# A spectral mix and a gated FFN on one core: half of the down projection by seven products, and a first product multiplied one step early

## The chip, the cores and the metric

The kernel runs on one core of a Trainium2 chip. The metric is the device time of one execution in microseconds (us). An engine is named by its short name: PE is TensorE, PEld its weight loads, ACT is ScalarE, DVE is VectorE, POOL is GpSimd, SP is SyncE, which here only issues DMAs.

## The reference, cut to what matters

Two stages follow each other. All arithmetic that the output sees is fp32.

```python
X = rfft(x, axis=1)                       # x: 8 batches x 3008 positions x 256
Yr = X.real @ w_r - X.imag @ w_i + b_r;  Yi = X.real @ w_i + X.imag @ w_r + b_i
Y  = softshrink(Yr, 0.01) + 1j * softshrink(Yi, 0.01)
y  = irfft(Y, n=3008, axis=1)             # 24064 tokens x 256
h  = y @ w_in                             # w_in: 256 x 2048
out = (h * sigmoid(1.702 * h)) @ w_out    # w_out: 2048 x 256
```

## The kernel before

**Numbers.** An fp32 operand is split into a high and a low part of a shorter format (`split`, L131: a cast on ACT, a subtraction on DVE), and a product of two operands is three matmuls into one PSUM bank (`mm3`, L134: high by high, high by low, low by high). This text calls such three matmuls a *product*.

**The spectral stage** (`spectral`, L256) makes y batch by batch: stage A, stage B, the mix with w_r and w_i, the inverse. Batch 0 is done ahead of the loop, in plain fp32. The first stages of batches 1 and 2 are a list called `filler`, taken two pairs at a time by `fill`. Everything later stands in `queue`, as steps with a cost each; the main loop takes the next step whenever the share of the costs spent lags behind the share of the way covered (L638). `tokens` (L425) turns y into tokens by features, eight small matmuls at a time, as soon as the loop will need them (L642).

**The FFN** is the main loop (L603). Tokens come in 24 tiles of 1024 (the last has 512), and the 2048 hidden features in eight blocks of 256: 192 steps, `k` the tile and `q` the block. In a step, the up projection of 256 hidden features from 256 inputs for 2 halves of 512 tokens is a 2 by 2 by 2 block product, and it is done with seven products instead of eight, by Winograd's form of Strassen's method. The seven turned weights of a block are made once, on DVE and ACT (`up_weights`, L220), stored in DRAM (`kept`), and loaded again for each later tile (`load_up`, L246). The seven token operands are made once per tile (`Tile`, L444). `Step.up` (L492) issues the products 1, 5, 6, 2, 7, 4, 3: products are added up in two banks, and ACT copies intermediate sums (`saved`, L478) that DVE adds to a later bank (`block`, L482, the addition in L486). Each of the four blocks of h gets its gate on ACT (L487) and is split.

The down projection of a step is eight plain products (`Step.down`, L518), accumulated over the eight steps of a tile in four PSUM banks `po`, which are copied out once per tile (L528). The downs of a step are multiplied during the step behind it. Four further PSUM banks (`bank()`) are shared by the up products and all of the spectral stage.

**The order** on each engine comes from a list scheduler that places instructions by the order of the program and by when buffers and operands come free in its own timeline; on the chip each engine's queue then runs in that fixed order. The order of the program around the change is set by one tuple, in which a number is an up product and 0 is one down product of the step before:

```python
PATTERN = (1, 5, 0, 6, 2, 0, 7, 0, 0, 4, 0, 3, 0, 0, 0)
```

The DMAs of the loop are all issued from SP; POOL issues the loads of the raw float64 weights (`from_float64`, L180).

## Time and profile before

| | us |
|---|---|
| median of 3 runs | 2602.62 (2600.95 to 2603.32) |
| the profiled execution | 2600.49 |
| span in its trace | 2598.4 |
| PE busy | 2550.3 (98%) |
| PE weight loads busy | 2129.2 (82%) |
| ACT busy | 1779.9 (69%) |
| DVE busy | 1551.5 (60%) |
| DMA moved | 376.33 MB, 145 GB/s |

The span runs from the first to the last instruction of the trace; the other 2.1 us of the profiled execution lie around it. Matmuls overlap in the trace: each is shown for longer than the distance to the start of the next, so what a matmul costs in a row of them is read from the starts. The same holds, in a smaller measure, for ACT and DVE.

### The profile page before, as it was taken

The numbers are of one execution on the slowest core, as the hardware profiler recorded it, in microseconds if no ns is written. First come the engines' busy times: TensorE is split into PE (matmuls) and PEld (weight loads), VectorE is DVE, ScalarE is ACT, GpSimd is POOL, SyncE is SP. The second block draws the span as 40 slices with busy tenths as digits, with TensorE's granted clock in tenths as the row PEclk, the third lists the DMA queues.
The fourth block names the chain that finished last, engine by engine and source line by source line (L and its number), as shares of the span: only waits on it lengthen the run. The fifth ranks groups of instructions, "written<-read, shape, count | busy, mean of one in ns | idle before, by whom it ended". The sixth has DMA issues, their size and how long they took to land.

```text
span 2598.4 us, 35299 instructions
## 1 busy us (share of the span) xinstructions
PE 2550.3 (98%) x12765; PEld 2129.2 (82%) x12765; DVE 1551.5 (60%) x2550; ACT 1779.9 (69%) x3309; POOL 13.8 (1%) x25
## 2 busy tenths in 40 slices
PE   6999999999999999999999999999999999999999
PEld 3768888888788888888878888788888888888888
DVE  5756665655556656566555665556656666455545
ACT  4577666666767668677676766767777676666667
POOL 1000000000000000000000000000000000000000
PEclk8899999999999999999999999999999999999999
DMA  9674544333544446343363444634355433433233
GB/s 298 196 228 131 166 133 132 128 122 118 177 133 138 131 135 201 128 141 125 128 201 115 140 127 152 193 105 144 120 171 168 131 126 117 137 121 120 86 105 124
DMA packets 183997, 376.33 MB, mean 145 GB/s; under 512 B 21808, under 2 KB 109232, under 8 KB 183824
## 3 DMA queue, kind: packets, MB, share of 16 engines
q1 hardware_dynamic: 181440, 365.70, 43.9%
q0 software_dynamic: 2384, 8.39, 1.1%
q8 instruction: 101, 1.65, 0.3%
q14 instruction: 72, 0.59, 0.1%
HBM read 266.52 MB, written 82.31 MB: 134 GB/s over the span
## 4 chain that ended last, share of the span: by engine, by line
PE 90%; DMA 5%; ACT 2%; DVE 1%; issue 1%; SPq 0%; ACTq 0%; POOL 0%; POOLq 0%
PE pa L135 15%; PE pa L136 14%; PE pa L137 14%; PE po L135 13%; PE po L136 12%; PE po L137 12%; PE pa L430 4%; PE pa L330 3%; DMA xr<-in_x 2%; PE pa L349 1%; PE pa L297 1%; DMA s<-aev 1%; DMA wraw<-in_w_in 1%; DMA yr<-mv 1%; ACT g L487 1%
## 5 line engine op out<-in xcount | busy, mean ns | idle before, releaser
L132 DVE TENSOR_TENSOR gl<-g,gl 128x512 fp32r<-128x512 f32 (+1 forms) x768 | 514.4, 676 | 336.1 <-ACT gl L132 333.4
L136 PE MATMUL po<-gl,wo_h 128*128 128x512 f32 (+1 forms) x1536 | 594.6, 388 | 0.0
L137 PE MATMUL po<-gl,wo_l 128*128 128x512 f32 (+1 forms) x1536 | 590.4, 385 | 0.0
L486 DVE TENSOR_TENSOR g<-pa,s 128x512 f32<-128x512 f32 (+1 forms) x576 | 387.0, 677 | 317.1 <-PE pa L137 227.5
L135 PE MATMUL pa<-tk,wq 128*128 128x512 f32 (+1 forms) x1344 | 536.7, 400 | 5.5 <-ACT iev L391 1.9
L136 PE MATMUL pa<-tk,wq 128*128 128x512 f32 (+1 forms) x1344 | 520.9, 388 | 0.0
L137 PE MATMUL pa<-tk,wq 128*128 128x512 f32 (+1 forms) x1344 | 518.8, 386 | 0.0
L487 ACT ACTIVATE g<-g 128x512 f32<-128x512 f32 (+1 forms) x576 | 358.3, 624 | 216.4 <-DVE g L486 214.3
L135 PE MATMUL po<-gl,wo_h 128*128 128x512 f32 (+1 forms) x1536 | 486.4, 390 | 1.6 <-ACT gl L132 1.2
L480 ACT COPY s<-pa 128x512 f32<-128x512 f32 (+1 forms) x576 | 330.0, 578 | 214.8 <-PE pa L137 208.9
L132 ACT CAST gl<-g 128x512 fp32r<-128x512 f32 (+1 forms) x768 | 464.0, 613 | 10.3
L136 PEld LDWEIGHTS po<-gl,wo_h 128*128 128x128 f32 x1536 | 288.9, 188 | 56.8 <-DVE gl L132 0.6
L137 PEld LDWEIGHTS po<-gl,wo_l 128*128 128x128 f32 x1536 | 288.8, 188 | 56.4 <-issue 0.7
L135 PEld LDWEIGHTS po<-gl,wo_h 128*128 128x128 f32 x1536 | 279.7, 188 | 58.2 <-ACT gl L132 6.3
L135 PEld LDWEIGHTS pa<-tk,wq 128*128 128x128 f32 x1344 | 254.0, 189 | 65.0 <-ACT s L480 8.4
L137 PEld LDWEIGHTS pa<-tk,wq 128*128 128x128 f32 x1344 | 253.4, 189 | 52.7 <-issue 0.5
L136 PEld LDWEIGHTS pa<-tk,wq 128*128 128x128 f32 x1344 | 254.3, 189 | 46.4 <-issue 2.9
L487 ACT ACTIVATE g<-pa 128x512 f32<-128x512 f32 (+1 forms) x192 | 112.8, 588 | 63.7 <-PE pa L137 62.3
L430 PEld LDWEIGHTS pa<-kc,ur 96*128 96x128 f32 x1024 | 139.5, 198 | 14.9 <-ACT we L200 2.7
L135 PE MATMUL pa<-wf_h,zh 128*128 128x256 f32 x504 | 143.4, 285 | 0.4 <-ACT g L487 0.3
L137 PE MATMUL pa<-wf_h,zl 128*128 128x256 f32 x504 | 142.4, 283 | 0.0
L136 PE MATMUL pa<-wf_l,zh 128*128 128x256 f32 x504 | 142.4, 282 | 0.0
(99 smaller groups left out, 2537.5 us busy)
## 6 DMA issues: line engine op xcount, KB each, us to landing
wq<-kept SPq DMA_DIRECT2D x184, 896.0 KB, 4.8
s<-aev SPq DMA_DIRECT2D x128, 192.0 KB, 3.1
br<-s SPq DMA_DIRECT2D x96, 256.0 KB, 3.3
yr<-mv SPq DMA_DIRECT2D x384, 64.0 KB, 2.0
s<-iev SPq DMA_DIRECT2D x96, 256.0 KB, 2.4
ur<-s SPq DMA_DIRECT2D x128, 192.0 KB, 3.4
out<-o SPq DMA_DIRECT2D x92, 256.0 KB, 2.8
xr<-in_x SPq DMA_DIRECT2D x80, 192.0 KB, 3.5
```

What stands on the lines that cost most here:

```text
L132: return nc.scalar.copy(hi, src).ins, nc.vector.tensor_tensor(lo, src, hi.bitcast(F32), ALU.subtract).ins
L135: nc.tensor.matmul(ps, lhsT=wh, rhs=xh, start=start, stop=False, skip_group_check=more)
L136: nc.tensor.matmul(ps, lhsT=wh, rhs=xl, start=False, stop=False, skip_group_check=more)
L137: nc.tensor.matmul(ps, lhsT=wl, rhs=xh, start=False, stop=stop, skip_group_check=more)
L297: done_a.append(nc.tensor.matmul(ps[:96], lhsT=ka32, rhs=xs.pop(q), start=True, stop=True).ins)
L330: nc.tensor.matmul(pv[:, c, :, i], lhsT=t[:, i, cs], rhs=k[:, i], start=True, stop=True)
L349: nc.tensor.matmul(ps, lhsT=z[:, 3 * c + v], rhs=wf32[v][:, c], start=c == 0, stop=c == 1)
L430: turned.append(nc.tensor.matmul(pv[:, c, 94 * j:94 * j + 94], lhsT=t[:, j, 128 * c:128 * c + 128], rhs=kz, start=True, stop=True).ins)
L480: nc.scalar.copy(t, ps[:, :self.w])
L486: nc.vector.tensor_tensor(t, ps[:, :w], self.s[other], ALU.add)
L487: nc.scalar.activation(t, ps[:, :w] if other is None else t, AF.Gelu_apprx_sigmoid)
```

## The change

Blocks 0 to 3 of the hidden features (`NF = 4`, a *fast* step) get a down projection by seven products; blocks 4 to 7 keep the eight plain ones.

- In a fast step, DVE makes four sums of the gated blocks (`block`: f5, f6, f7, f4). Four of the seven products (1, 5, 6, 7) are multiplied as the step's downs. Their sums over the four fast steps stand in the four `po` banks.
- After the downs of step 3 the banks are turned (`Tile.turn`): four copies on ACT and four additions on DVE, with PSUM as source and destination, combine the four banks.
- The other three products (2, 3, 4) go straight into the turned banks. Their operands are kept in fp32 (`held`, a pool of 12 buffers), and split and multiplied one fast step at a time among the downs of the plain steps 4 to 7 (`tile.solo`), which thus have 11 products.
- The downs of a step are still multiplied during the next one, so the pattern has two forms: with four downs (`FEW`, in steps 1 to 4) and with eleven (`MANY`, in steps 5, 6, 7 and 0).
- The up products come in the order 1, 6, 2, 5, 7, 3, 4. Product 1 of a step is multiplied within the step in front of it, and ACT copies it from its bank into the bank that the step in front has just emptied (a PSUM to PSUM copy); product 2 is added onto it there. One addition on DVE per step is gone with that, and the bank goes on being used.
- Turned weights of w_out for the fast blocks are made, stored and loaded like those of w_in, in halves (`HALVES`: u, v of w_in, d, e of w_out; four tiles of buffers for halves of four, four for halves of three).
- The costs of the spectral queue are spread unevenly over the steps of a tile (`SHARE`), and tokens are wanted between steps 4 and 6.9 of a tile, where it was 2.5 to 6.5.
- The copies out of the four banks are made together after the last down of a tile (`Tile.finish`).

```diff
+NF = 4
+TK, GL, G, WQ, DF = 7, 6, 5, 4, 3 * NF
+HALVES = {"u": (1, 6, 2, 5), "v": (7, 3, 4), "d": (1, 5, 6, 7), "e": (2, 3, 4)}
...
+    def load_turned(h, n):
         k, q = divmod(n, NQ)
+        if k < NT and (k or h == "e") and q < (NF if h in "de" else NQ):
+            nc.sync.dma_start(flat(new_turned(k, h, q)), kept[h, q])
...
+        def turn(self):
+
+            c11, c12, c21, c22 = (self.bank(m, n) for m in range(2) for n in range(2))
+
+            def add(to, ps):
+                t = buf2("tn").rearrange("p c d -> p (c d)")[:, :self.w]
+                nc.scalar.copy(t, ps)
+                for o in to:
+                    nc.vector.tensor_tensor(o, o, t, ALU.add)
+
+            add((c12,), c11)
+            add((c21,), c12)
+            add((c12,), c22)
+            add((c22,), c21)
...
         def block(self, name, ps, other=None):
             w = self.w
-            t = buf([128, TOK], F32, "g", bufs=G)[:, :w]
+            t = held(w) if self.fast and name[0] else buf([128, TOK], F32, "g", bufs=G)[:, :w]
             if other is not None:
                 nc.vector.tensor_tensor(t, ps[:, :w], self.s[other], ALU.add)
             nc.scalar.activation(t, ps[:, :w] if other is None else t, AF.Gelu_apprx_sigmoid)
...
+            if not self.fast:
+                self.cut(name, t)
+            elif name == (0, 0):
+                self.cut(1, t)
+            elif name == (0, 1):
+                f[5], f[6] = (buf([128, TOK], F32, "g", bufs=G)[:, :w] for _ in range(2))
+                v.tensor_tensor(f[5], t, f[0, 0], ALU.subtract)
+                self.cut(5, f[5])
+                v.tensor_tensor(f[6], f[1, 1], f[5], ALU.subtract)
+                self.cut(6, f[6])
+                v.tensor_tensor(t, t, f[1, 1], ALU.subtract)
+                self.cut(7, t)
+            elif name == (1, 0):
+                f[4] = held(w)
+                v.tensor_tensor(f[4], f[6], t, ALU.subtract)
 
         def up(self, p):
+            w = self.w
             if p == 1:
                 self.a = bank()
                 self.product(1, self.a, True, True)
-                self.saved("p1", self.a)
+                if self.b is None:
+                    self.saved("p1", self.a)
+                else:
+                    nc.scalar.copy(self.b[:, :w], self.a[:, :w])
             elif p == 5:
                 self.c = bank()
                 self.product(5, self.c, True, True)
+                self.saved("p5", self.c)
+            elif p == 2:
...
+                    self.product(2, self.b, False, True)
+                    self.block((0, 0), self.b)
             elif p == 6:
                 self.product(6, self.a, False, True)
                 self.saved("u2", self.a)
+            elif p == 3:
+                self.product(3, self.c, False, True)
+                self.block((0, 1), self.c, "u2")
             elif p == 7:
                 self.product(7, self.a, False, True)
-                self.saved("u3", self.a)
-                self.block((1, 1), self.c, "u3")
+                self.block((1, 1), self.a, "p5")
...
+    BLOCKS = ((0, 0), (0, 1), (1, 1), (1, 0))
+    FEW = (6, 2, 0, 5, 7, 0, 3, 1, 0, 4, 0)
+    MANY = (6,0,2,0,5,0,7,0,0,3,0,0,0,4,0,1,0,0)
+    SHARE = (1.6,.3,.3,.3,.5,1.6,1.7,1.7)
...
+        if n < NF - 1:
+            turn_weights(1, n + 1, True)
+        if n < NQ - 3:
+            turn_weights(0, n + 3, True)
+        if q < NF:
+            load_turned("d", n)
+        else:
+            load_turned("e", n - NF)
+        load_turned("u", n + 2)
+        load_turned("v", n + 2)
...
+        pattern = FEW if 1 <= q <= NF else MANY
+        for i, p in enumerate(pattern):
+            if p == 1:
+                if n + 1 < NT * NQ:
+                    follow = Step(coming if last else cur, (q + 1) % NQ, step)
+                    follow.up(1)
+            elif p:
                 step.up(p)
                 if last:
                     coming.factor(p)
-            elif behind:
-                behind.pop(0)()
+            else:
+                next_down()
```

## Rows read from the trace of the kernel before

**Rows 1.** The page's first part: the span, then busy time and share of it for each engine, with instructions.

```profile
span 2598.4 us, 35299 instructions
PE 2550.3 (98%) x12765; PEld 2129.2 (82%) x12765; DVE 1551.5 (60%) x2550; ACT 1779.9 (69%) x3309; POOL 13.8 (1%) x25
```

**Rows 2.** The page's fourth part: the chain of work that ended last, by engine.

```profile
PE 90%; DMA 5%; ACT 2%; DVE 1%; issue 1%; SPq 0%; ACTq 0%; POOL 0%; POOLq 0%
```

**Rows 3.** Busy time by stretches. The first four are each about one tile of the main loop, from its first up product on: the first tile, one in the middle, one of those behind the last batch's spectral work, and the last, of half the width. The fifth is the last step of the first tile. Columns: the stretch and its length, busy us (instructions) of PE, PEld, DVE, ACT and POOL, granted clock, DMA share, GB/s.

```profile
127.70:259.70 132.00, 129.38 (x588) 95.81 (x587) 85.20 (x163) 95.14 (x184) 2.15 (x4) 0.98 0.56 179
1229.40:1342.40 113.00, 109.87 (x533) 89.90 (x532) 65.77 (x106) 80.04 (x150) 0.00 (x0) 1.00 0.48 150
2290.30:2376.40 86.10, 86.10 (x401) 72.02 (x400) 44.46 (x69) 56.75 (x103) 0.00 (x0) 1.00 0.33 110
2545.30:2598.40 53.10, 49.21 (x383) 47.71 (x381) 27.10 (x65) 36.29 (x97) 0.00 (x0) 0.98 0.40 135
...
239.80:259.70 19.90, 18.75 (x108) 15.68 (x107) 15.66 (x26) 15.80 (x30) 0.00 (x0) 1.00 0.30 84
```

**Rows 4.** Groups of instructions in the third of these stretches (one tile without spectral work): busy us, mean ns of one, idle time before.

```profile
L480 ACT COPY s<-pa 128x512 f32<-128x512 f32 x24 | 14.1, 589 | 10.7 <-PE pa L137 10.2
L430 PE MATMUL pa<-kc,ur 96*128 96x94 f32 x40 | 5.3, 270 | 0.0
```

**Rows 5.** PE in order of time, start and shown length in us: matmuls of 512 columns, then of 256 columns in the last tile.

```profile
2299.79 0.39 PE L135 MATMUL pa<-tk,wq 128*128 128x512 f32 x1
2300.02 0.39 PE L136 MATMUL pa<-tk,wq 128*128 128x512 f32 x1
2300.25 0.39 PE L137 MATMUL pa<-tk,wq 128*128 128x512 f32 x1
2300.47 0.39 PE L135 MATMUL pa<-tk,wq 128*128 128x512 f32 x1
...
2581.25 0.28 PE L135 MATMUL pa<-tk,wq 128*128 128x256 f32 x1
2581.37 0.28 PE L136 MATMUL pa<-tk,wq 128*128 128x256 f32 x1
```

**Rows 6.** DVE in order of time: instructions back to back, and one behind a wait (idle time before it and what ended it, in brackets).

```profile
203.12 0.69 DVE L132 TENSOR_TENSOR gl<-g,gl 128x512 fp32r<-128x512 f32 x1 [1.57 <-ACT gl L132]
203.73 0.68 DVE L486 TENSOR_TENSOR g<-pa,s 128x512 f32<-128x512 f32 x1
204.33 0.68 DVE L132 TENSOR_TENSOR tk<-y,tk 128x512 fp32r<-128x512 f32 x1
...
2301.35 0.69 DVE L486 TENSOR_TENSOR g<-pa,s 128x512 f32<-128x512 f32 x1 [1.03 <-PE pa L137]
```

**Rows 7.** ACT in order of time, in the same form.

```profile
204.94 0.65 ACT L487 ACTIVATE g<-g 128x512 f32<-128x512 f32 x1
205.47 0.60 ACT L487 ACTIVATE g<-pa 128x512 f32<-128x512 f32 x1
205.95 1.15 ACT L132 CAST gl<-g 128x512 fp32r<-128x512 f32 x2
...
2298.89 0.63 ACT L132 CAST gl<-g 128x512 fp32r<-128x512 f32 x1
2299.41 0.60 ACT L528 COPY o<-po 128x512 f32<-128x512 f32 x1
2299.89 0.62 ACT L487 ACTIVATE g<-pa 128x512 f32<-128x512 f32 x1
2300.67 0.59 ACT L480 COPY s<-pa 128x512 f32<-128x512 f32 x1 [0.17 <-PE pa L137]
...
2302.08 0.63 ACT L487 ACTIVATE g<-g 128x512 f32<-128x512 f32 x1 [0.30 <-DVE g L486]
```

**Rows 8.** Who waited for whom on PE's weight loads, whole span: us in total, times, longest.

```profile
PEld pa L135 <- ACT s L480: 8.4, 24, 1.1
PEld po L135 <- ACT gl L132: 6.3, 11, 0.8
PEld pa L135 <- DVE g L486: 5.9, 11, 1.4
```

**Rows 9.** In order of time, POOL's loads of raw weights for the blocks that are turned inside the loop, two loads per block, and DVE's last splits of turned weights.

```profile
125.58 1.13 POOL L198 DMA_DIRECT2D wraw<-in_w_in  x2 [13.47 <-DVE w L237]
146.14 1.13 POOL L198 DMA_DIRECT2D wraw<-in_w_in  x2 [19.43 <-DVE w L237]
163.39 1.07 POOL L198 DMA_DIRECT2D wraw<-in_w_in  x2 [16.12 <-DVE w L237]
...
208.42 1.15 DVE L132 TENSOR_TENSOR wq<-w,wq 128x512 fp32r<-128x512 f32 x2
```

**Rows 10.** DMA issues of the turned weights: count, KB each, median us from issue to landing.

```profile
wq<-kept SPq DMA_DIRECT2D x184, 896.0 KB, 4.8
```

**Rows 11.** SP in order of time: the stores at the end.

```profile
2594.05 1.80 SPq L530 DMA_DIRECT2D out<-o  x4
```

**Rows 12.** The mix of the spectral stage, whole span: one of its three groups of matmuls, and one of the two DVE additions that empty its two banks.

```profile
L136 PE MATMUL pa<-wf_l,zh 128*128 128x256 f32 x504 | 142.4, 282 | 0.0
...
L355 DVE TENSOR_TENSOR mv<-pa,mv 128x512 f32<-128x512 f32 x96 | 66.1, 688 | 50.6 <-PE pa L137 45.1 <-PE pa L349 4.2
```

More of the change, by code (lines that the diff above doesn't have):

```diff
@@ L225, in up_weights @@
         if spare:
-            w = [buf([128, 4, 128], F32, "w4", tag="sl") for _ in range(2)]
+            w = [buf([128, 4, 128], F32, "wt", tag="sl") for _ in range(2)]
         else:
@@ L596, in fourier_mix_then_gated_ffn @@
         fill(1)
-    for q in range(NQ):
-        weights(q)
+    for i in range(4 + NQ - NF):
+        weights(i)
     cur = Tile(0)
@@ L601, in fourier_mix_then_gated_ffn, with prepare, next_down, progress @@
         cur.factor(p)
-    behind, total = [], None
+    behind, ready, closing, total, step = [], [], None, None, None
+    def prepare(count):
+        while behind and len(ready) < count:
+            get, run = behind.pop(0)
+            ready.append((get(), run))
+    def next_down():
+        nonlocal closing
+        prepare(3)
+        if ready:
+            g, run = ready.pop(0)
+            run(g)
+        if closing and not ready and not behind:
+            closing()
+            closing = None
+    def progress(part):
+        n = int(part)
+        k, q = divmod(n, NQ)
+        return NQ * k + sum(SHARE[:q]) + SHARE[q] * (part - n)
     for n in range(NT * NQ):
         k, q = divmod(n, NQ)
-        if n < NQ - WQ:
-            up_weights(WQ + n, True)
-        load_up(n + 2)
+        if n < NF - 1:
[4 more added lines that the diff above has]
+            load_turned("d", n)
+        else:
+            load_turned("e", n - NF)
+        load_turned("u", n + 2)
+        load_turned("v", n + 2)
         last = q == NQ - 1 and k + 1 < NT
@@ L610, in fourier_mix_then_gated_ffn @@
             coming = Tile(k + 1)
-        step = Step(cur, q)
-        extra = []
+        if n == 0:
+            step = Step(cur, 0, None)
+            step.up(1)
+        if last:
+            coming.factor(1)
         if not queue and nextb < NB:
@@ L646, in fourier_mix_then_gated_ffn @@
                 tokens_to(need)
-        behind = [lambda f=f, h=h, m=m, step=step: step.down(f, h, m) for f, h in BLOCKS for m in range(2)]
+        while behind or ready:
+            next_down()
+        behind = step.down()
+        if q == NF - 1:
+            closing = cur.turn
+        elif q == NQ - 1:
+            closing = cur.finish
+        step = follow
         if last:
             cur = coming
-    for do in behind:
-        do()
+    while behind or ready:
+        next_down()
 def kernel(x, w_r, w_i, b_r, b_i, moe_w_in, moe_w_out):
```

203 lines of the change are left out of this document (117 added, 86 removed).

## The prediction, made before the change was run

> **What bounds the kernel now.** I read the shares first: PE is busy for 98% of the span, ACT for 69%, DVE for 60% [rows 1]. A busy PE need not be a full one, so next the chain of waits: 90% of it is PE work, 5% DMA, 3% ACT and DVE [rows 2]. Then the stretches by tile. The reader is to see that a tile without spectral work is a sum of matmuls and nothing else [rows 3]: matmuls of 512 columns start 0.227 us apart ((2300.47 - 2299.79) / 3), those of 256 columns 0.12 apart [rows 5]; a tile has 8 x 45 = 360 of the FFN and 40 small ones of the tokens, (86.1 - 360 x 0.227) / 40 = 0.11 us each [rows 4], so its 86.1 us hold no gap. With spectral work a tile takes 113 us and PE is still shown busy for 109.9. So a matmul taken out anywhere behind the start is worth its 0.227 us, as long as ACT, DVE and the weights keep up.
>
> What reserve do they have? Their shown lengths overlap. Back to back, DVE instructions of 512 start 0.60 us apart (203.12, 203.73, 204.33), though each is shown as 0.69. On ACT a cast costs 0.52 (2298.89 to 2299.41), a copy 0.48, a gate 0.53 from SBUF and 0.48 from PSUM (204.94, 205.47, 205.95) [rows 6, 7]. By these prices the 69 DVE instructions of the gapless tile are 41 us of its 86, its 103 on ACT about 52 [rows 3].
>
> **The change, part by part.** *Products.* A tile has eight steps with 7 up products. Before, 8 x 8 = 64 downs; after, 4 x 4 in the fast blocks and 4 x 11 in the plain ones, 60 in all. That is 12 matmuls less per tile: 23 x 12 x 0.227 + 12 x 0.12 = 64.1 us off PE. The trace shows the price both with and without spectral work beside it; in a tile with it a matmul costs a little more, so 64 is if anything low.
>
> By the Trainium skill, "TensorE: Matmul & The Clock Gate" (Back-to-back issue gap), a matmul of 512 columns costs N/2.4 + 2.5, or 216 ns; the same sum would then be 61 us. The trace differs, with 227 ns at a granted clock of 1.00, and decides.
>
> *ACT and DVE, whole.* A step loses one DVE addition of three. A fast step gains four sums; a tile gains 12 splits of the late operands (a cast and a subtraction each) and four copies and four additions for the turn. Per tile: DVE - 8 + 16 + 12 + 4 = + 24, so 93 x 0.60 = 56 us of some 83; ACT + 16, so about 60 of 83. In copies per step ACT is where it was (P1, u2, p5 for p1, u2, u3). The seed copy writes PSUM, which no row shows; the nearest row is the copy from PSUM to SBUF at 0.589 [rows 4], and I take that, with an addition's 0.69 as the upper end and 0.4 as the lower; on ACT alone the difference hides. So in the mean neither engine becomes the bound: cost 0, hidden behind PE. Without that cover the 24 x 0.60 would be 14 us per tile.
>
> *The lean stretch.* What is true of the mean need not be so of steps 1 to 4, which have 11 products each: 33 x 0.227 = 7.49 us. DVE has two additions, four sums, four splits, 10 x 0.60 = 6.0; ACT 3 copies, 4 gates, 4 casts, 5.5. With a share of 0.3 of the spectral work the load is alike: DVE near 80%, ACT near 75%. Both fit, but there is a new closed circle. Product 3 of a step fills a bank, DVE adds u2 to it (which empties it), ACT gates that sum, ACT copies P1 of the next step into the emptied bank, and only then may product 6 of the next step go on in P1's bank, and product 2 in the seeded one. Its length by rows: a reader starts 0.42 after the start of the last matmul (2300.25 to 2300.67), 0.19 after that one's slot; addition 0.69 and 0.04 to hand on (2301.35 + 0.69 to 2302.08); the gate ahead of the copy 0.53; the copy 0.59 [rows 5 to 7]. Sum 2.05 us. FEW has four products between 3 and the next 6 (1, 0, 4, 0), 12 x 0.227 = 2.72. So 0.67 us is left, about one instruction in front on either engine. Queued behind a late product 6 on PE is everything, as it works in order. Before, a copy had to be ready in the time of two products, and PE lost 8.4 us to it in 24 waits [rows 8]. I take 0.1 us for each of 92 seams: + 9 (between 0 and the rival below).
>
> *The turn* adds a wait for the plain downs of step 5. Its last piece is one addition, one copy and one addition after product 7 of step 3's downs, 0.19 + 0.69 + 0.59 + 0.69 with hand-overs, 2.3 us (no row shows an addition with PSUM on both sides; the nearest reads PSUM and one SBUF operand at 0.69 [rows 6], and 0.5 to 1.0 would move the sum by 0.4 us a tile at most). The first down into a bank that still has to be turned is the third of MANY, after products 6, 0, 2, 0, 5: 3.4 us. What may be in front of it on ACT and DVE leaves 1.1: + 3 (0 to 25, one us per tile).
>
> *DMA and SP.* 92 loads of 512 and 92 of 384 KB are new, 85 MB; the 896 KB of old become 512 and 384. One of 896 KB lands in 4.8 us [rows 10], and a lean step of 8 us asks for one and a half such; the middle tile uses 48% of the DMA engines [rows 3]. Each load is issued a step or more ahead. Some 370 more issues at 0.45 (1.80 / 4 [rows 11]) are 165 us of SP, which has none on the path: 0.
>
> *The first tile.* Weights are turned in the loop through one set of buffers: the next block's raw load waits until DVE is done with the sums of the one before, and such loads stand 20.6 and 17.3 us apart [rows 9]. Before, five blocks went this way, the last load at 163.4; now eight (three of w_out, five of w_in), so the last at about 163.4 + 3 x 17 = 215, plus, at the least, the 45 us that the last one took from its load to its split (163.4 to 208.4) less the 15 or so that it stood waiting for a free weight tile, about 245. Step 7 began at 240 before [rows 3], and its product 1 is now wanted earlier. Ahead of the loop four plain splits give way to one turned block, beside PE: 0. So the first tile doesn't get its 2.7 us and I add + 6 (0 to 20).
>
> *The end.* In the half tile a lean step has 33 x 0.12 = 4.0 us on PE, and the circle (shown lengths of 0.42 and 0.37) some 1.4 us against 4 x 0.36: + 1. The four copies out come after the last product instead of in between, and then four issues of 0.45: + 2. Together + 3 (1 to 6).
>
> *Banks.* Before, up products held two of the four `pa` banks for most of a step; now two all the time, and three for a part of each lean step, as the seeded bank lives across the seam. The spectral work, moved to MANY steps, has two. PE has FFN products to go on with while one drains: 0 here (the rival has its price).
>
> Sum: - 64.1 + 9 + 3 + 6 + 3 = - 43. The profiled execution took 2600.5, that makes 2557.4; the median of the runs lies 2.1 above it, so **2560 us**.
>
> **The rivals.** *The seam decides (the slower side).* DVE and ACT are at 80% in the lean stretch, and each works in a fixed order. If two DVE instructions and one cast stand in front, the circle is 2.05 + 2 x 0.60 + 0.52 = 3.77 and PE stands for 1.05 us at each of 92 seams, 97 us instead of 9: 2648. It decides from (43 + 9) / 92 = 0.57 us per seam; above that the change costs time. For it: the sums of a fast step (f5, f6, f7 and their splits) are ready just behind the addition and run into the next step. Against it: 1.5 us of each lean step are free on DVE, and MANY steps enter the stretch without a backlog.
>
> *The banks.* A mix takes two banks at once, 18 matmuls x 0.12 = 2.2 us to fill and then two additions of 0.69 [rows 5, 12]. With two left, the next spectral product waits for these, 1.3 us. With 84 mixes behind batch 0 this is 109 us if nothing else is in the order there; if FFN products cover four fifths, 22 us: 2582. For it: DVE waits for PE there and not the other way [rows 12], so a mix is drained as soon as it is full, but into a DVE that is now fuller. Against it: the up products of MANY need no new bank between 5 and 1. By the Trainium skill, "Perfetto Trace Analysis" (Optimization Strategy), the same gap repeating on the engine that should be full can mean too little PSUM for the next tile. The trace before shows no such gap.
>
> *All of it arrives,* and the waits of PE [rows 8] (20.6 us) go too, since what PE waits for now is further ahead: 2602.6 - 64 - 15 = 2524 at the best, 2533 with the first tile and the end.
>
> *The change doesn't do what it says:* the four products less are saved, but the weights come late and a lean step ends with its loads, 1408 KB at 896 / 4.8 = 187 KB per us, 7.5 us, if they can't overlap, against 7.49 of PE. With the spectral loads beside them 8.5: + 1 us x 69, 2629. The loads do overlap in the first tile (179 GB/s at 56% [rows 3]), so I hold little of it.
>
> **How the numbers follow.** Forecast (2540 to 2576) 0.52; banks, or a little of several waits (2576 to 2597), 0.23; all of it (under 2540) 0.08; the seam 0.13, of which about a third ends near no change; late weights 0.04. The range leaves out the best few hundredths and the larger part of the seam: 2537 to 2604; the likeliest case has 2540 to 2576. A measurement tells 0.2%, 5 us, from no change. Faster 0.81, the same 0.06, slower 0.13.
>
> **What would show it.** Right: 288 matmuls less on PE; tiles without spectral work near 83.5 us; PE's share still over 96%; DVE near 75%, ACT near 77%. Waits of PE's weight loads for the seed copy (ACT, line of the PSUM to PSUM copy) would show the seam, hundreds of times if the rival is right. Waits before the first product of a spectral stage for the gates or DVE's additions show the banks. A first tile that ends past 260 shows the weights. Wrong would be a span that shrinks without fewer matmuls to match, or lean steps of over 9 us.

## The result, and the profile after

The change made the kernel slower by half a per cent: 2614.89 us (median of 5 runs, 2612.28 to 2622.13) against 2602.62 (2600.95 to 2605.76), ratio 1.0052, 95% interval 1.0039 to 1.0064. Forecast was 2560, with 2537 to 2604 as the range. The page of the changed kernel, its first part and the chain by engine, answers to [rows 1, 2]:

```profile
span 2612.8 us, 37190 instructions
...
PE 2523.4 (97%) x12477; PEld 2080.2 (80%) x12477; DVE 1889.0 (72%) x3173; ACT 1939.9 (74%) x3706; POOL 14.9 (1%) x28
...
PE 81%; DMA 6%; ACT 5%; DVE 2%; issue 1%; SPq 1%; ACTq 0%; POOL 0%; DVEq 0%; POOLq 0%
```

The 288 matmuls are gone (12765 to 12477), as forecast. Yet PE's busy time fell by only 26.9 us, and its time outside it rose from 48.1 (2598.4 - 2550.3) to 89.4. The first number already holds a trap: a matmul is shown for 0.39 us and followed 0.227 later, so that a wait of up to 0.16 us still looks busy, and at the half clock everything is busy. I therefore counted from the starts of all matmuls in the trace: the distance to the next start, less the median distance for that line and shape, where the rest is over 0.03 us; stretches at the half clock apart.

```
us                          before   after   difference
waits of PE                   82.1    145.1     +63.0
  before 118 us               26.1     22.4      -3.7
  118 to 400 (two tiles)      17.4     32.5     +15.1
  400 to 2150                 34.9     76.0     +41.1
  behind 2150                  3.7     14.2     +10.5
excess at the half clock      20.6     36.1     +15.5
```

78.5 us more against 64 us fewer: the two kernels' profiled spans differ by 14.4. So nothing was wrong with the saving; 76 us of new waits (64 + 12 by the medians) have to be found. Where they are by tile, the stretches of the changed kernel show (same form as [rows 3]): the first tile, the one that answers to the middle tile of [rows 3], one without spectral work, the last, and one in the middle in which a batch begins.

```profile
126.00:273.30 147.30, 135.43 (x580) 97.75 (x580) 112.08 (x233) 108.30 (x212) 5.36 (x10) 0.92 0.69 228
...
1247.10:1361.90 114.80, 110.32 (x517) 87.73 (x516) 79.86 (x128) 88.10 (x169) 0.00 (x0) 0.99 0.62 190
2305.00:2388.70 83.70, 83.67 (x389) 69.74 (x388) 60.16 (x94) 63.59 (x119) 0.00 (x0) 1.00 0.51 157
2555.10:2612.40 57.30, 51.20 (x382) 48.55 (x380) 36.00 (x90) 39.32 (x114) 0.00 (x0) 0.99 0.54 177
918.10:1037.50 119.40, 114.59 (x534) 92.36 (x533) 81.17 (x133) 90.25 (x170) 0.00 (x0) 0.97 0.61 184
```

The tile without spectral work came out at 83.7 us, forecast 83.5, with no gap. A tile with spectral work did not: 114.8 where 113.0 was [rows 3], 119.4 where the same tile before took 108.9. These two are among the worse ones: from the third tile to the nineteenth, 17 in all, the mean by the starts of their up products is 106.9 us, and 106.8 before. So in the mean such a tile gave back its whole saving of 2.7 us and no more. The first took 147.3 instead of 132.0. And DVE is busy for 80 us of the middle tile (66 before), ACT for 88 (80): by the shares there is still a quarter free.

Who PE waited for, whole span, in the form of [rows 8]:

```profile
PEld po L137 <- ACT gl L134: 17.0, 31, 2.5
...
PEld pa L137 <- ACT pa L577: 15.8, 28, 1.8
PEld pa L137 <- ACT g L550: 14.6, 21, 1.8
...
PEld pa L137 <- ACT aev L320: 10.1, 10, 2.4
PEld pa L137 <- ACT wu L134: 9.8, 2, 7.4
PEld pa L137 <- ACT xh L134: 9.2, 7, 2.8
```

The reader is to see that no line rules (the two left out, of 16.6 and 11.6 us, are the plain stage A of the first three batches, where before it was 15.7 and 13.5). Before, the three largest waits of the loop were 8.4, 6.3 and 5.9 us [rows 8]; now there are six of 9 to 17, in 2 to 31 events each, and all are ACT: the splits of the gated blocks (gl), the seed copy (L577), the gates (L550), the copies of stage A (aev), the turned weights (wu), the cast of x (xh). The same gap does not repeat: the largest of them is 17 of 145 us.

How such an event comes about is seen at 998 us, in order of time on ACT, DVE and PE:

```profile
997.68 0.62 ACT L134 CAST xh<-xr 96x512 fp32r<-96x512 f32 x1 [2.02 <-DMA xr<-in_x]
998.21 0.61 ACT L134 CAST gl<-g 128x512 fp32r<-128x512 f32 x1
...
998.33 0.69 DVE L134 TENSOR_TENSOR xl<-xr,xh 96x512 fp32r<-96x512 f32 x1 [10.35 <-ACT xh L134]
...
998.35 0.48 PE L137 MATMUL pa<-xh,ka 96*96 96x512 f32 x1 [2.37 <-ACT xh L134]
998.87 0.50 PE L137 MATMUL po<-gl,wo_h 128*128 128x512 f32 x1
...
1000.61 0.63 PE L137 MATMUL pa<-xh,ka 96*96 96x512 f32 x1
```

ACT's next instruction is a cast of x whose load has not landed; it stands for 2.02 us, and behind it the splits that the downs need. DVE, in its own fixed order, has stood for 10.35 us, PE for 2.37. Two microseconds on, matmuls start 0.42 apart: the granted clock is at its lower level, 1.2 GHz, for 3.4 us. None of the three engines was full. Late loads of x are nothing new. ACT's waits for them, before and after, are

```profile
ACT xh L132 <- DMA xr<-in_x: 35.2, 24, 3.5
```

```profile
ACT xh L134 <- DMA xr<-in_x: 29.4, 29, 3.2
```

and so no longer in sum than before; but PE's weight loads waited 3.6 us for the cast then, in 3 events, and wait 9.2 in 7 now. I read this as lost room: what hid a late load before no longer does.

### The profile page after: what moved, and what is told of

It reads as the page before. It is cut to its first block, busy times and chain, and to the rows that moved or that the text cites. A ratio compares the mean times of both kernels' runs of the same rounds, so it can differ in the third digit from the quotient of the medians.

```text
span 2612.8 us, 37190 instructions
## 1 busy us (share of the span) xinstructions
PE 2523.4 (97%) x12477; PEld 2080.2 (80%) x12477; DVE 1889.0 (72%) x3173; ACT 1939.9 (74%) x3706; POOL 14.9 (1%) x28
## 4 chain that ended last, share of the span: by engine, by line
PE 81%; DMA 6%; ACT 5%; DVE 2%; issue 1%; SPq 1%; ACTq 0%; POOL 0%; DVEq 0%; POOLq 0%
PE pa L137 14%; PE pa L138 13%; PE pa L139 13%; PE po L137 11%; PE po L138 11%; PE po L139 11%; PE pa L449 4%; PE pa L349 3%; DMA xr<-in_x 2%; DMA wd<-kept_d 2%; ACT g L550 1%; DMA yr<-mv 1%; PE pa L316 1%; ACT gl L134 1%; DMA ur<-s 1%
## 5 line engine op out<-in xcount | busy, mean ns | idle before, releaser
L134 DVE TENSOR_TENSOR gl<-g,gl 128x512 fp32r<-128x512 f32 (+1 forms) x768 | 511.8, 675 | 191.1 <-ACT gl L134 187.1
L137 PE MATMUL pa<-tk,wu 128*128 128x512 f32 (+1 forms) x768 | 311.3, 405 | 20.4 <-ACT wu L134 9.0
L138 PE MATMUL pa<-tk,wu 128*128 128x512 f32 (+1 forms) x768 | 300.1, 391 | 0.0
L139 PE MATMUL pa<-tk,wu 128*128 128x512 f32 (+1 forms) x768 | 299.9, 391 | 0.0
L138 PE MATMUL po<-gl,wo_h 128*128 128x512 f32 (+1 forms) x768 | 298.6, 389 | 0.0
L139 PE MATMUL po<-gl,wo_l 128*128 128x512 f32 (+1 forms) x768 | 295.8, 387 | 0.0
L540 ACT COPY s<-pa 128x512 f32<-128x512 f32 (+1 forms) x385 | 217.1, 585 | 105.0 <-PE pa L139 102.4
L137 PE MATMUL po<-gl,wo_h 128*128 128x512 f32 (+1 forms) x768 | 291.1, 396 | 3.4 <-ACT gl L134 3.0
L549 DVE TENSOR_TENSOR g<-pa,s 128x512 f32<-128x512 f32 (+1 forms) x289 | 195.3, 677 | 100.7 <-PE pa L139 74.2
L550 ACT ACTIVATE g<-g 128x512 f32<-128x512 f32 (+1 forms) x289 | 180.1, 624 | 102.2 <-DVE g L549 100.0
L137 PE MATMUL pa<-tk,wv 128*128 128x512 f32 (+1 forms) x576 | 228.9, 397 | 0.3 <-DVE g L549 0.2
L134 DVE TENSOR_TENSOR gl<-df,gl 128x512 fp32r<-128x512 f32 (+1 forms) x288 | 194.1, 674 | 45.5 <-ACT gl L134 45.1
L138 PE MATMUL pa<-tk,wv 128*128 128x512 f32 (+1 forms) x576 | 222.1, 386 | 0.0
L139 PE MATMUL pa<-tk,wv 128*128 128x512 f32 (+1 forms) x576 | 222.0, 385 | 0.0
L134 ACT CAST gl<-df 128x512 fp32r<-128x512 f32 (+1 forms) x288 | 178.1, 618 | 26.9 <-PE po L139 25.7
L137 PEld LDWEIGHTS pa<-tk,wu 128*128 128x128 f32 x768 | 146.0, 190 | 63.8 <-ACT pa L577 15.8
L550 ACT ACTIVATE g<-pa 128x512 f32<-128x512 f32 (+1 forms) x287 | 172.0, 599 | 24.5 <-PE pa L139 22.1
L139 PEld LDWEIGHTS pa<-tk,wu 128*128 128x128 f32 x768 | 145.8, 190 | 31.6 <-issue 0.8
L137 PEld LDWEIGHTS po<-gl,wo_h 128*128 128x128 f32 x768 | 143.2, 190 | 34.3 <-ACT gl L134 8.7
L138 PEld LDWEIGHTS po<-gl,wo_h 128*128 128x128 f32 x768 | 145.6, 190 | 29.2 <-DVE gl L134 0.5
```

What stands on the lines that cost most here:

```text
L134: return nc.scalar.copy(hi, src).ins, nc.vector.tensor_tensor(lo, src, hi.bitcast(F32), ALU.subtract).ins
L137: nc.tensor.matmul(ps, lhsT=wh, rhs=xh, start=start, stop=False, skip_group_check=more)
L138: nc.tensor.matmul(ps, lhsT=wh, rhs=xl, start=False, stop=False, skip_group_check=more)
L139: nc.tensor.matmul(ps, lhsT=wl, rhs=xh, start=False, stop=stop, skip_group_check=more)
L540: nc.scalar.copy(t, ps[:, :self.w])
L549: nc.vector.tensor_tensor(t, ps[:, :w], self.s[other], ALU.add)
```

## The experiments

Each run stands beside runs of the kernel before on the same chip (2601.3 to 2602.0 us). "e4" is the base of many of them.

**Taking the change apart.** e1: the seven products, with product 1 back in its own step. e2: product 1 early and seeded, without the seven products. e15: product 1 early, but saved to SBUF and added on DVE as before, without the seven products. e4: the same with the seven products, which is the changed kernel without the seed.

```diff
# e4
-            self.b = prev.c if prev else None
+            self.b = None
...
-                if self.b is None:
-                    self.saved("p1", self.a)
-                else:
-                    nc.scalar.copy(self.b[:, :w], self.a[:, :w])
+                self.saved("p1", self.a)
# e1: besides, Step(cur, q, None) in every step, and
+    FEW = (1, 5, 0, 6, 2, 0, 7, 3, 0, 4, 0)
+    MANY = (1, 5, 0, 0, 6, 2, 0, 0, 7, 0, 0, 3, 0, 0, 4, 0, 0, 0)
# e2, e15: besides (e2 keeps the seed)
+NF = 0
+    MANY = (6, 0, 2, 0, 5, 0, 7, 0, 0, 3, 0, 4, 0, 1, 0)
+    SHARE = (1., 1., 1., 1., 1., 1., 1., 1.)
```

> Seven products in four of eight blocks, as changed, but product 1 of a step is multiplied in its own step, saved to SBUF and added on DVE as before (one more DVE addition per step, and the bank of product 3 comes free within its step). The spread of the spectral work and the weights are those of the changed kernel. Theory 'seam' (the seeded bank that lives across the step costs the spectral stage its banks, some 45 us): 2570 to 2580, and PE's waits for a gate or an evacuation before an up product fall to the level of before. Theory 'bunching' (the spectral work pressed into four steps meets its own DMA and ACT latencies): 2605 to 2620, stage A's waits stay.

> Eight plain products in every block as before, even spread of the spectral work as before, but product 1 early and seeded. Theory 'seam': 2635 to 2650 (before plus some 45). Theory 'bunching': 2598 to 2608, no difference from before, DVE some 115 us less busy.

> The changed kernel, product 1 still multiplied a step early, but saved to SBUF and added on DVE; product 2 gets a bank of its own. Theory 'seam': the bank of product 3 comes free in its step, so 2575 to 2590. Theory 'bunching': 2615 to 2625 (one DVE addition more per step, nothing gained).

> No seven products at all: eight plain products in every block as before the change, P1 of the next step early and saved to SBUF (e2 without the seed). If seven products have given back all that they save, early P1 alone makes the whole gain of e4: 2591 (2586 to 2594). If seven products with early P1 are worth something, it is above e4: 2600, or, with e2's 2641 less the 24 of the seed and the held bank, 2617.

Measured: e1 2600.65 us, ratio 0.9995 (0.9984 to 1.0006); e2 2641.13, 1.0160 (1.0145 to 1.0175); e4 2591.00, 0.9964 (0.9952 to 0.9976); e15 2595.99, 0.9984 (0.9975 to 0.9993). So the seven products in themselves give back all that they save, with product 1 in its own step (e1) or, but for 5 us, early (e15 to e4). Product 1 a step early is worth 5.7 us (e15 against 2601.7), together with what else of the change e15 keeps: the order of the up products, weights loaded in halves, the copies out of the four banks made together. The seed with its bank costs 23.9 us beside seven products (e4 to after) and 45 beside eight (e15 to e2).

Where part of the 45 is, PE's weight loads show, first e15, then e2:

```profile
PEld pa L137 <- ACT s L540: 7.2, 14, 1.1
PEld pa L137 <- ACT g L550: 7.2, 14, 1.5
```

```profile
PEld pa L137 <- ACT g L550: 22.8, 28, 2.5
PEld pa L137 <- ACT pa L577: 20.2, 33, 1.7
PEld pa L137 <- ACT s L540: 4.5, 11, 0.6
```

The line L540 is three copies of a step to SBUF in e15 and two in e2, where the third is the seed copy to PSUM (L577). So the three make PE wait 17.5 us longer (20.2 + 4.5 - 7.2), and the gates 15.6. By the program, a seeded bank is emptied by an ACT gate, where an unseeded one is emptied by DVE's addition.

**The seed.** e5 is e4 with product 2 put into the bank of product 3 of the step in front, as in the changed kernel, but without the copy: it holds the bank across the seam. e12 gives product 6 one product more of cover, by moving a down product in front of it. e13 moves the copy from ACT to DVE.

```diff
# e5, in up(2) of e4
-                    b = bank()
+                    b = self.hold if self.hold is not None else bank()
# e12, in the changed kernel
-    FEW = (6, 2, 0, 5, 7, 0, 3, 1, 0, 4, 0)
-    MANY = (6,0,2,0,5,0,7,0,0,3,0,0,0,4,0,1,0,0)
+    FEW = (0, 6, 2, 5, 7, 0, 3, 1, 0, 4, 0)
+    MANY = (0,6,2,0,5,0,7,0,0,3,0,0,0,4,0,1,0,0)
# e13, in the changed kernel
-                    nc.scalar.copy(self.b[:, :w], self.a[:, :w])
+                    nc.vector.tensor_copy(self.b[:, :w], self.a[:, :w])
```

> Product 1 early, saved to SBUF and added on DVE as in the run before this one (2591 us), but product 2 goes into the bank that product 3 of the step in front has filled, so that this bank is held across the seam as in the changed kernel, with no seed in it. Theory 'bank held': 2608 to 2620, as slow as the changed kernel, with up products and spectral products waiting for a gate that frees a bank. Theory 'seed copy' (products 6 and 2 wait for a copy that itself waits for DVE's addition): 2586 to 2598, as fast as the early product without the seed.

> The changed kernel with its seed, one down product moved ahead of product 6, so that five products instead of four lie between product 3 and the product that waits for the seed copy. Theory 'circle too short' (2.05 us plus one or two instructions against 2.72): 0.68 us more cover takes back most of the 17 us that the copy costs, 2595 to 2604. Theory that the copy costs elsewhere (its place in ACT's order, PSUM held): 2608 to 2618.

> The changed kernel whole, but the seed copy from bank to bank is done by DVE, right behind the addition that empties the bank, instead of by ACT. DVE then has as many instructions as in e4 (the copy stands where the addition of P1 stood), ACT one copy less per step. If the seed costs its 17 us because the copy stands in ACT's order and holds up the casts and gates behind it, the time falls to that of e5, 2597 (2593 to 2602). If the price lies in the dependence itself (products 6 and 2 of the next step wait for a copy that waits for an addition), or if DVE is the scarcer engine, it stays at 2615 or rises to 2630.

Measured: e5 2597.57, 0.9987 (0.9977 to 0.9998); e12 2620.16, 1.0065 (1.0050 to 1.0080); e13 2621.00, 1.0068 (1.0055 to 1.0082). Of the 23.9 us the held bank has 6.6 and the copy 17.3; by the intervals of the ratios each is good to about 4 us. Two explanations of the 17 found no support. More cover for product 6 did not help (e12): PE's weight loads wait 16.4 us for the copy in 27 events, much as the 15.8 in 28 below, so a circle that is short by up to a product is not what these waits are. Nor does the copy's place in ACT's order explain them: on DVE, PE waits half as long for the copy,

```profile
  PEld pa L137: 8.0, 13
```

where in the changed kernel the same line of the same group (L577, who waited for it) is

```profile
  PEld pa L137: 15.8, 28
```

and the time is no shorter. What does move is in front of the spectral stage. Weight loads of stage A (pa<-xh,ka) and what they waited for, e4 and then the changed kernel:

```profile
  ACT xh L134: 10.4, 12
  ACT aev L320: 4.0, 6
  ACT g L550: 1.8, 2
  DVE g L549: 0.5, 2
```

```profile
  ACT xh L134: 9.2, 7
  ACT aev L320: 9.1, 7
  ACT g L550: 5.4, 7
  ACT y L457: 1.0, 1
```

The wait for the cast of x is nearly the same; the waits for a bank that ACT has yet to empty went from 6.3 (the three lower lines) to 15.5. At the mix they went from 0.8 (a copy of tokens, an addition) to 5.9 (5.0 of it gates). In e5 they are 10.7 and 2.4, but its profiled execution took 2588.6 us, 9 less than its median, so that this trace can't say where the 6.6 us lie. So waits of 14 us, beside a loss of 24, are seen as banks that come free late. Why a copy that holds no further bank makes it so I did not settle: each kernel is laid out anew by the scheduler, and its order on ACT differs.

**How the spectral work is spread.** e3 is the changed kernel with all shares 1; e8 is e4 with the shares drawn together; e9 is e4 with three pairs of `filler` instead of two in the lean steps.

```diff
# e3
+    SHARE = (1., 1., 1., 1., 1., 1., 1., 1.)
# e8
+    SHARE = (1.4, .5, .5, .5, .7, 1.4, 1.5, 1.5)
# e9
-                fill(2)
+                fill(3 if pattern is FEW else 2)
```

> The changed kernel with its spectral work spread evenly over the eight steps of a tile; nothing else. Theory 'bunching': 2565 to 2580, as the 45 us of added waits in the middle tiles go. Theory 'seam', or that the lean steps are filled by DVE and ACT: 2615 to 2640, worse than the change, with the waits now in steps 1 to 4.

> Product 1 early and saved to SBUF (2591 us), with the spectral work spread less unevenly: 1.4, .5, .5, .5, .7, 1.4, 1.5, 1.5. Theory 'bunching': 2575 to 2587, stage A's waits in steps 6 and 7 fall. Theory that the lean steps have no room: 2592 to 2605, waits move into steps 1 to 4.

> Early product 1 without the seed (2591 us), with three instead of two portions of the first batches' stage A at a time in the lean steps of the first tile, as many per product as before. Theory 'lean first tile' (its short steps 1 to 3 outrun the turning of weights, PE stands 10 us and loses its clock): 2573 to 2584, no wait of 7 us for a turned weight near 195 us. If the turning takes the same time anyway and only the order changes: 2588 to 2594.

Measured: e3 2634.70, 1.0128 (1.0112 to 1.0143); e8 2605.48, 1.0011 (0.9999 to 1.0022); e9 2598.41, 0.9989 (0.9975 to 1.0003). The bunching of the spectral work is not the loss; any more work in the lean steps costs 7 to 20 us (e9 and e8 against e4, e3 against the changed kernel; e9 moves `filler`, which ends within the first tile). These steps have no room, though the mean of either engine says that they have.

**The added work.** e10 is e4 in which the fast blocks are multiplied by the plain weights that stay in SBUF: no turned weights of w_out are made, stored or loaded. e11 is e4 without the 16 sums and the 12 late splits of a tile. e14 is both.

```diff
# e10
-                wd = turned_w.pop((tile.k, "d", q))
...
-                    mm3(tile.bank(m, n), wd[:, 0, i], wd[:, 1, i], *g, start=q == 0, stop=False, more=True)
+                    ms = slice(128 * m, 128 * m + 128)
+                    mm3(tile.bank(m, n), wo_h[:, q, i % 2, ms], wo_l[:, q, i % 2, ms], *g, start=q == 0, stop=False, more=True)
...
-        if q < NF:
-            load_turned("d", n)
-        else:
-            load_turned("e", n - NF)
# e11
-                v.tensor_tensor(f[5], t, f[0, 0], ALU.subtract)
-                self.cut(5, f[5])
-                v.tensor_tensor(f[6], f[1, 1], f[5], ALU.subtract)
-                self.cut(6, f[6])
-                v.tensor_tensor(t, t, f[1, 1], ALU.subtract)
-                self.cut(7, t)
+                self.cut(5, t)
...
-                tile.solo.append(((self.f[1, 0], 0, 0), (self.f[1, 1], 0, 1), (self.f[4], 1, 0)))
+                tile.solo.append((((0, 0), 0, 0), ((0, 1), 0, 1), ((1, 1), 1, 0)))
```

> Early product 1 without the seed, and the seven products of the fast blocks take slices of the plain resident weights in place of turned ones (left out: turning, storing and loading of w_out's four blocks, 86 MB of loads; the products, the sums and their splits stay). Theory 'weights and DMA': the first tile loses its 20 us and the loads' waits go, 2560 to 2575. Theory 'ACT and DVE' (the sums, the late splits): 2580 to 2590, only the first tile gains.

> Early product 1 without the seed, without the four sums of a fast step and without the splits of the late operands (left out: 16 sums and 12 splits per tile; their products take operands that are there). PE's products and all loads stay. Theory 'ACT and DVE' (fuller engines answer PE later in the middle tiles, some 30 us): 2555 to 2570. Theory 'weights and DMA': 2583 to 2592.

> e10 and e11 in one: P1 early and saved, the fast blocks multiplied by the plain weights kept in SBUF (so no turning, storing or loading of w_out's turned weights), and without the 16 sums and 12 late splits per tile; both parts of the output are left out. If the weights' price (37 us) and the engines' price (31 us) are separate, they add up: 2591 - 68 = 2523 (2517 to 2529). If both are the same waits seen from two sides, the time stays near the better of the two, 2540 to 2554.

Measured: e10 2553.79, 0.9810 (0.9796 to 0.9825); e11 2560.41, 0.9832 (0.9815 to 0.9848); e14 2541.67, 0.9772 (0.9759 to 0.9785). The weights cost 37.2 us, the sums and splits 30.6, both together 49.3, 18.5 us less than their sum: the two prices overlap. Where they lie, the tiles show, taken from the start of one tile's product 6 to the next. In the 17 tiles from the third to the nineteenth, either has 1.3 us per tile, 22 us; the first tile has 15.3 us of e10's 37.2 (145.3 in e4, 130.0 in e10) and 3.8 of e11's. The shares of e4 and then of e11 say what hides behind a mean:

```profile
PE 2509.8 (97%) x12477; PEld 2076.4 (80%) x12477; DVE 1987.0 (77%) x3364; ACT 1945.1 (75%) x3706; POOL 14.9 (1%) x28
```

```profile
PE 2503.9 (98%) x12477; PEld 2077.6 (81%) x12477; DVE 1612.4 (63%) x2692; ACT 1794.6 (70%) x3418; POOL 14.9 (1%) x28
```

DVE goes from 77 to 63%, ACT from 75 to 70%, neither was a bound at either level, and the kernel is 30.6 us shorter. e11 leaves out two things at once, the instructions and the chain in which products 5, 6 and 7 wait for the sums; which of the two held PE up, no run tells apart. e10's 22 us in the middle tiles come with DVE and ACT as busy as in e4 (77 and 76%), so they are not the price of more instructions there. By the Trainium skill, "Perfetto Trace Analysis" (Optimizing Scalar/DVE Operations), ScalarE and VectorE can cause bubbles on other engines without being saturated; here that is 1.2% of the kernel.

**The turning inside the first tile.** e6 is the changed kernel in which the blocks to be turned within the loop are not turned, but loaded as the turned block 0 (which is therefore stored earlier); e7 is the same with the kernel before.

```diff
# e6 (e7 alike, with its one tile of seven)
+        if spare:
+            for h in "de" if d else "uv":
+                to = new_turned(0, h, q)
+                nc.sync.dma_start(flat(to), kept[h, 0])
+                fresh.append((-1 if h == "e" else q + d, h, q, to))
+            return
...
-                keep_turned(-1, stored[15])
+                keep_turned(1, stored[15])
```

> The changed kernel, but the eight blocks of weights that are turned inside the loop are not computed: the turned tile of block 0 is loaded in their place (left out: raw loads, ACT's and DVE's work on them in the first steps). Theory 'weights' (the first two tiles are held up by turning): first tile 20 us shorter, whole 2586 to 2598. If turning hides: 2608 to 2616, first tile as before.

> The kernel before with the same left out: its five blocks turned inside the loop are loaded as block 0. Theory 'weights': the five hide behind PE, 2594 to 2602; so the difference to the run above is the price of the three blocks of w_out. If it gains as much as the changed kernel does, the turning is no part of the loss.

Measured: e6 2610.87, 1.0038 (1.0024 to 1.0053); e7 2597.12, 0.9984 (0.9975 to 0.9994). The computing of turned weights costs about 4 us in both kernels, and in e6 that is hardly clear of noise. But the first tile's loss is a matter of late weights all the same. The changed kernel has two waits of PE in it for turned weights of w_in, at product 1 of steps 4 and 5:

```profile
173.75 0.56 PE L137 MATMUL pa<-tk,wu 128*128 128x512 f32 x1 [2.01 <-ACT wu L134]
...
195.54 0.80 PE L137 MATMUL pa<-tk,wu 128*128 128x512 f32 x1 [6.98 <-ACT wu L134]
```

In e6 the loads that stand in their place come no earlier, and PE waits for these instead:

```profile
PE pa L137 <- DMA wv<-kept_v: 6.2, 1, 6.2
PE pa L137 <- DMA wu<-kept_u: 4.4, 1, 4.4
```

So e6 changed what PE waits for, and not that it waits. The kernel before and e7 have no such wait. In the changed kernel the raw loads of w_out's blocks take turns with those of w_in, and block 5, for which the second wait is, has its raw load issued at 174.53; before, that was at 125.58 [rows 9]. Just in front of its cast, ACT stands for the raw load of the block behind it:

```profile
163.55 1.07 POOL L200 DMA_DIRECT2D wraw<-in_w_out  x2 [18.09 <-ACT pa L577]
174.53 1.07 POOL L200 DMA_DIRECT2D wraw<-in_w_in  x2 [9.91 <-DVE wt L248]
...
192.12 0.43 ACT L202 ACTIVATE we<-wraw 128x256 f32<-128x256 f32 x1 [2.50 <-DMA wraw<-in_w_in]
```

Around and behind the two waits the granted clock is at 1.2 GHz for 20.5 us (174.0 to 177.4, 191.1 to 208.2). Counted from the starts of the matmuls, the first tile has 22.6 us of waits and an excess of 11.1 at the lower clock, where before it had 13.2 and 2.0. e10, which turns no weights of w_out, waits 0.6 us for turned weights in that tile, has the higher level in it from 132 us on, and runs through it in 130.0 us, e4 in 145.3.

**SP's queue.** In the changed kernel SP stands in front of weight loads until PE is done with a tile of weights (its two largest waits):

```profile
SPq L269 <- PE pa L139: 679.8, 310, 9.5
SPq L269 <- PE po L139: 343.2, 134, 7.8
```

That is 1023 us in 444 waits, with loads of x, stores and all else of the spectral work behind it in order; before it was 783 in 160. How long SP stands there does not go with the time of the kernel, though: e15 (2595.99 us) has 1030 us in 307 waits, e10 (2553.79) 932 in 301. e17 issues the weight loads from POOL's queue, with no other edit. They are 556 loads by the page, and not the 464 of the expectation; by its third part, 263 MB then move in the queue called software_dynamic, 8.4 MB in the changed kernel.

```diff
-            nc.sync.dma_start(flat(new_turned(k, h, q)), kept[h, q])
+            nc.gpsimd.dma_start(flat(new_turned(k, h, q)), kept[h, q])
```

> The changed kernel whole, with one edit: the loads of turned weights (464 per run) are issued from POOL's queue, which is empty behind the first tile, instead of SP's. In the changed kernel SP stands for 1023 us in front of these loads, 444 times, until PE is done with a weight tile, and the loads of x, the stores and the other transfers of the spectral work stand behind it in order. If the 37 us that go with w_out's turned weights are this queue (transfers of the spectral work issued late, ACT's cast and stage A waiting for them), the time falls by 20 us or more, to 2595 or less. If they are the DMA engines' load, the weights' own landing, or the spectral work's own order, it stays at 2615 (2608 to 2620).

Measured: 2636.52, 1.0131 (1.0114 to 1.0149). The gain did not come: the waits moved to POOL, and the kernel lost 22 us more. Since the loads changed the kind of their queue as well, e17 alone can't rule out SP's order; with e10 and e15 beside it, nothing measured speaks for it. In its trace SP stands elsewhere instead (691 us where 192 were),

```profile
SPq L384 <- DVE mv L377: 690.9, 76, 18.0
```

and PE's wait for the splits of the downs is 21.4 us where it was 17.0. Why it is slower was not followed further.

**A middle way.** e16 is e4 with two fast blocks instead of four; e18 is that with the loads on POOL's queue.

```diff
-NF = 4
+NF = 2
...
-        pattern = FEW if 1 <= q <= NF else MANY
+        pattern = FEW if 1 <= q <= NF else MANY if NF < q <= 2 * NF else MID
+    MID = (6, 0, 2, 0, 5, 0, 7, 0, 0, 3, 0, 4, 0, 1, 0)
+    SHARE = (1.1, .3, .3, 1.4, 1.5, 1.1, 1.1, 1.2)
```

> e4 with two fast blocks of eight instead of four (36 products and half of the turned weights, sums and late splits). If the costs grow in proportion, it lies halfway between e15 and e4, 2591 to 2604. If they rise faster than in proportion, because each engine has room for the first few and none for the rest, it beats both: 2570 to 2585.

> e16 (two fast blocks, P1 early and saved) with the same edit, the loads of turned weights from POOL's queue: the candidate for the best version. If SP's queue holds up the spectral work there as well, 2560 to 2572; if not, 2581 as e16 (2577 to 2585).

Measured: e16 2581.27, 0.9925 (0.9913 to 0.9937); e18 2596.61, 0.9985 (0.9976 to 0.9994). e16 is the best version found, 20 us faster than the kernel before and 34 faster than the changed one. With 0, 2 and 4 fast blocks and product 1 early without a seed: 2595.99, 2581.27, 2591.00, for savings of 0, 32 and 64 us. So the price of the seven products is 17 us for two blocks and 59 for four: more than in proportion, each with a pattern and shares of its own (e16's were drawn for two blocks).

## Why the prediction was wrong, point by point

Put together, with medians: 2602.6 before, - 64.1 for the matmuls, - 5.7 for product 1 early, is 2532.8. e14, which has these, the lean steps and the turn, measured 2541.7; the 8.9 between are not taken apart. Then + 49.3 for w_out's weights and for the sums and splits (e14 to e4), + 6.6 for the held bank (e4 to e5), + 17.3 for the seed copy (e5 to the changed kernel): 2614.9.

- *Products, - 64.1.* Right: 288 matmuls went, and the tile without spectral work takes 83.7 us (forecast 83.5). The 216 ns that the prediction set beside its 227 are given by the Trainium skill, "TensorE: Matmul & The Clock Gate" (Back-to-back issue gap), for a matmul by itself; the sum did not use them.
- *ACT and DVE, whole: "neither becomes the bound: cost 0, hidden behind PE".* This is the step that failed, with the next one. The shares came out near the forecast (DVE 72, ACT 74%; 75 and 77 were named), neither became the bound, and still the sums and late splits cost 30.6 us alone (e11). The argument took a mean share for room. The event at 998 us shows how PE comes to wait all the same, when one of the fixed orders is late at one place. That added instructions make an order late at more places is my reading of e11, which also shortens the chain to the products; it is not shown by itself. The gapless tile from which I took the prices has no spectral work, and in such tiles the step did hold.
- *DMA and SP, 0.* w_out's turned weights cost 37.2 us alone (e10), 49.3 together with the one above. Of the 37.2, 15.3 lie in the first tile, where another term had the mechanism (below), and 22 in the middle tiles, for which the prediction had nothing. PE waits for w_out's loads themselves for few of them (6.6 us, 6 times). What share of the 22 goes through the DMA engines, the weight tiles or the order on ACT was not told apart; no run speaks for SP's queue, which I would have named first.
- *The lean stretch, + 9.* The seam cost 23.9 (0.26 us at each of 92, where I had put 0.1). The term was too small, and its mechanism is not borne out: no gain by more cover (e12), 28 waits for the copy and not hundreds. The rival "The seam decides" needed 0.57 us per seam, so it did not come true either, although the time ended on its side.
- *Banks, 0; rival 22.* Its mechanism is in the trace: stage A waits 15.5 us and the mix 5.9 for banks not yet emptied, in e4 6.3 and 0.8, in the kernel before 2.5 and 1.4. The rival had their size about right, yet put them down to the mix filling two banks, where stage A has most. By the Trainium skill, "Perfetto Trace Analysis" (Matmuls), independent groups of matmuls should rotate through different banks so that emptying one overlaps the next; e5 agrees, a bank held across a seam cost 6.6 us.
- *The first tile, + 6.* It lost 15.3 us (147.3 against 132.0) where the sum had + 3.3 (6 less its share of 2.7). The mechanism that I named, weights turned late because w_out's blocks stand between those of w_in, is the one in the trace. But it struck earlier than at step 7, the product that waited was the early product 1 of steps 4 and 5, and it cost more than twice the 6: two waits of 9.0 us together, and the lower clock behind them. Without w_out's weights the 15 are gone (e10 against e4).
- *The end, + 3.* The last tile took 57.3 us, from product 6 on, against 53.1 before. Fifteen matmuls of 0.12 less (three of them product 1, which now lies ahead) and the forecast 3 more would be 54.3, so it is 3.0 over.
- *The turn, + 3* was not measured alone.

The signs named for "right" came (288 matmuls less, 83.7 us, PE's share 97%, DVE 72 and ACT 74%, each 3 points under the forecast) although the forecast was wrong: a share of PE that shows waits as work, and means of the helpers, could not have told. The signs that did speak were those of the waits, stage A's and the first tile's, which ended at 273 where 260 had been named. The chance given to the slower side, 0.13, was too small because each cause was asked whether it alone would cost 43 us. None did; several of 7 to 37 us did so together.

## What to carry to other kernels

When PE is at 98% and its helpers at 60 to 70%, work moved to the helpers is not free: here 28 more instructions on DVE and 12 on ACT for each tile of some 107 us cost PE 1.3 us per tile at a DVE share under 80%. Every engine runs in a fixed order, and a delay at one place can reach PE, as at 998 us, while the mean still shows room. Price added work by a run that leaves out only that work, or by a tile in which all the other work is going on, and not by a gapless stretch. And try the change at half its size: the saving grew in proportion, the price faster, and two fast blocks beat both none and four.

## What the runs showed of the hardware that was not expected

A copy from PSUM to PSUM on ACT is shown at 0.581 us in the median, the copy from PSUM to SBUF at 0.589 in the same trace (the middle one of the three durations):

```profile
L577 ACT COPY pa<-pa x191: 357/581/646, 140.3 to 2597.1; 128x512 f32<-128x512 f32 x183, 128x256 f32<-128x256 f32 x8
```

```profile
L540 ACT COPY s<-pa x385: 365/589/697, 127.4 to 2599.4; 128x512 f32<-128x512 f32 x185, 128x256 f32<-128x256 f32 x8
```

On DVE the same copy is shown at 0.694. So my nearest row, 0.589, was within 0.01 us for an operation that the trace before did not have. By the Trainium skill, "ScalarE: Activation LUTs" (Step-by-step: what each stage is for), writing PSUM is faster for ScalarE than writing SBUF; for these tiles the trace agrees by 8 ns, too little to plan with.
